# Sliding-window attention with ALiBi, then an ELU feed-forward: the order of the first steps, the layout of q and k, and the store of the last 128 rows

## Chip, core and metric

One NeuronCore of a Trainium2 chip runs the whole program. The metric is the device time of one execution in microseconds (us); lower is better. TensorE (PE) does the matmuls, VectorE (DVE), ScalarE (ACT) and GpSimd (POOL) the elementwise work, and SyncE (SP) issues some of the DMAs.

## The reference, cut to what matters

```python
# q, k, v: [8 batches, 8 heads, 576 positions, 64], f32; w_in [512, 2048]; w_out [2048, 512]
scores = (q @ k.T) / 8
rel  = pos[:, None] - pos[None, :]
bias = slopes[head] * -abs(rel)               # slopes = 2 ** -(head + 1) for 8 heads
mask = (rel >= 0) & (rel < 128)               # each query sees itself and the 127 keys before it
attn = softmax(where(mask, scores + bias, -1e9))
x = (attn @ v), heads side by side            # [4608 tokens, 512]
h = x @ w_in                                  # [4608, 2048]
g = where(h > 0, h, exp(min(h, 0)) - 1)       # ELU
out = g @ w_out                               # [4608, 512], f32
```

## The kernel before

**Tiling.** A batch has 576 positions: four blocks of 128 and a tail of 64. Because of the window a block of queries needs only its own block of keys and the one before it. Positions inside the first 512 are permuted by the load, so that long runs of memory land on each partition. All inputs come in on POOL's DMA queue and are cast to f16 on the way. Scores are computed with keys on the partitions and queries on the free axis, so their exponentials can serve directly as the stationary operand of the matmul with v; v carries a column of ones (`VW = D + 2`), which gives the softmax denominators.

**Layout.** `QK[i]` (two buffers, by the batch's parity) holds q and k with the head dimension on partitions 0 to 63: `[128, 2, 5, H, 128]`, that is q or k, then block, then head, then position. Partitions 64 to 127 hold extra rows of terms, the same for all batches, whose products add the ALiBi bias and large negative numbers outside the window. They are made once in `QK[1]` (`terms` L235 to L245 and `group_rows` L249 to L254 make `TQ` and `TK`; `fill_q` L257 on ACT, `fill_k` L261 on POOL and `k_term` L266 on DVE spread them over the heads) and are copied to `QK[0]` by one DMA (`fill_other` L270). Batch 0 does not wait for them: its scores use 64 rows only and add the bias by a second matmul of `cI` with `DM` (L372).

**Attention in banks.** A batch is 16 steps. `scores(b, s)` fills one PSUM bank (L352), and ACT takes its exponential (L376); for batches from 1 on DVE then clips outside the window (`cut`, L384); `values(b, s)` multiplies with v one step later (L398); `normalize` divides (L418, L419); `turn` brings the result into `xT`, with tokens on the free axis (L432 and L434 for batches 0 and 1, a transposing DMA after that).

**How q and k get into QK.** Batch 0 is loaded in two halves of 256 positions (`load_half`, L90), and each half is transposed on PE for four heads at a time (`transposes_half`, L291): `transposes_half(a, hq)` is half `a`, heads `4 hq` to `4 hq + 3`, 16 transposes, 8 of k and 8 of q. Batch 1 is loaded whole (`load_qk`, L83) and transposed for two heads at a time (`transposes`, L310, four calls at steps 13, 14, 15, 15). `put` (L300) copies each of these PSUM tiles into QK in two copies, both by one engine: DVE, or ACT where the last argument is true. Later batches go through DVE's 32x32 transpose (`squares`, L321) and gathering DMAs of SP (`collect`, L327). The 64 tail positions of each batch come by `load_tail` (L104, one DMA for k and one for q) and go through `transposes_tail` (L335, copies L340); for batch 0 that is in step 12, for batch 1 in step 25.

**Feed-forward.** It runs behind the attention in the same loop over steps. `hidden` computes 512 columns of `x @ w_in` (L455), ACT takes exp (L459), POOL limits it to at most 1 (L460); `elu` combines both on DVE one step later (L467); `output` accumulates `g @ w_out` (L496), ACT copies the bank (L500), SP stores it (L502). Each bank of hidden values is used by every second step, so `hidden` of step s + 2 waits for `elu` of step s. The first `hidden` is in step 4, the first `output` in step 13.

**Order.** It is written out by hand (`tc.manual_schedule()`): `at(s, f, ...)` appends `f` to step s, and the loop at the end emits, for each step, `hidden`, `elu` of the bank before, the tasks in the order in which they were appended, and `output`. Every engine runs its own instructions in that order. `warm(n)` (L509) issues n matmuls on the identity that nobody reads. Before step 0 stand `warm(34)`, the transposes of batch 0's first half for all heads, `warm(12)`, and `place_v4(0, 0)` (L119, DVE copies of v); each of steps 1 to 4 begins with `warm(8)`. `place_by_pool` (L124) does the rest of v's placing on POOL.

**POOL's DMA order.** Ahead of the loop: k, q (half 0), v (half 0), w_in 0 and 1, k, q (half 1), v (half 1), w_in 2 and 3, w_out 0 and 1. In the loop: k of batch 1 (step 4), q of batch 1 (step 5), w_out 2 and 3 (steps 6 and 7), tail of k and tail of q of batch 0 (steps 8 and 9), tail of v of batch 0 (step 10), v of batch 1 (step 11), and so on.

**The end.** The last four groups of 128 rows (`output` with t = 8) run on PE alone once the hidden values are done. The last group's 128 rows lie in three pieces of the output (`rows_of`: 32, 32 and 64 rows), so SP issues three stores after ACT's last copy.

Of the kernel before, what the change touches and what calls it, by code (L numbers as in the profile page):

```python
# [19 lines left out]
def kernel(  # L20
# [48 lines left out]
    QK = [one([128, 2, 5, H, 128], F16, f"QK{i}") for i in range(2)]  # L69
# [69 lines left out]
    with tc.manual_schedule():  # L139
# [68 lines left out]
        def zeros():  # L208
            for i in range(2):
                V.memset(QK[i][0:64 + 64 * i, 1, 4, :, 64:128], 0.0)  # L210
                V.memset(VP[i][64:128, 4, :, 0:D], 0.0)
            for e in EX:
                V.memset(e[:, 512:576], 0.0)
# [19 lines left out]
        def terms():  # L233

            V.tensor_scalar(out=is96, in0=rowf, scalar1=96.0, scalar2=None, op0=ALU.is_equal)  # L235
            V.tensor_scalar(out=is97, in0=rowf, scalar1=97.0, scalar2=None, op0=ALU.is_equal)
            V.tensor_scalar(out=isx, in0=is97, scalar1=-1.0, scalar2=None, op0=ALU.mult)
            V.tensor_scalar(out=pm[r_, :], in0=posi[r_, :], scalar1=float(-MID), scalar2=None,
                            op0=ALU.add)
            V.tensor_scalar(out=TQ[r_, 0:576], in0=pm[r_, :], scalar1=isx[r_, :], scalar2=is96[r_, :],  # L240
                            op0=ALU.mult, op1=ALU.add)
            V.tensor_scalar(out=TK[r_, 0:576], in0=pm[r_, :], scalar1=is96[r_, :],
                            scalar2=is97[r_, :], op0=ALU.mult, op1=ALU.add)
            for t in (TQ, TK):
                V.memset(t[64:128, 576:640], 0.0)  # L245
# [10 lines left out]
        def fill_q(n):  # L256
            nc.scalar.copy(QK[1][64:128, 0, n, :, :],  # L257
                           TQ[64:128, 128 * n:128 * n + 128].unsqueeze(1).broadcast_to([64, H, 128]))

        def fill_k(n):  # L260
            nc.gpsimd.tensor_scalar(  # L261
                out=QK[1][g_, 1, n, :, :], in0=TK[g_, 128 * n:128 * n + 128].unsqueeze(1)
                .broadcast_to([32, H, 128]), scalar1=1.0, scalar2=0.0, op0=ALU.mult, op1=ALU.add)

        def k_term(h):
            V.tensor_scalar(out=QK[1][r_, 1, :, h, :], in0=TK[r_, :].rearrange("p (n c) -> p n c", c=128),  # L266
                            scalar1=8.0 * 2.0 ** (-8.0 * (h + 1) / H), scalar2=None, op0=ALU.mult)
# [13 lines left out]
        def transposes_half(a, hq):  # L281

            if a:
                t = ps_o.tile([128, 2, 2, 4, 2, 32], F16, name="tph", tag="op")
            else:
                t = ps_s.tile([128, 2, 2, 4, 2, 32], F16, name="tp", tag="sps")
            p = slice(64 * a, 64 * a + 64)
            for w in (1, 0):
                for g in range(4):
                    for j in range(2):  # L290
                        nc.tensor.transpose(  # L291
                            t[:, w, :, g, j, :],
                            stq[0][p, w, 4 * hq + g, 2 * j:2 * j + 2, :].rearrange("p a d -> p (a d)"),
                            ident[p, p])
            put(t, QK[0][0:64, :, 2 * a:2 * a + 2, 4 * hq:4 * hq + 4, :], hq and not a)

        def put(t, o, by_act):

            for odd in range(2):
                (nc.scalar.copy if by_act else V.tensor_copy)(  # L300
                    o.rearrange("p w n h (a o i) -> p w n h a o i", o=2, i=32)[:, :, :, :, :, odd, :]
                    .rearrange("p w n h a i -> p w n (h a) i"),
                    t[64 * odd:64 * odd + 64].rearrange("p w n h a i -> p w n (h a) i"))

        def transposes(b, hp):
            t = ps_s.tile([128, 2, 4, 2, 2, 32], F16, name="tp", tag="sps")
            for g in range(2):
                for w in (1, 0):
                    for j in range(2):
                        nc.tensor.transpose(  # L310
                            t[:, w, :, g, j, :],
                            stq[b][:, w, 2 * hp + g, 2 * j:2 * j + 2, :].rearrange("p a d -> p (a d)"),
                            ident)
            put(t, QK[b % 2][0:64, :, 0:4, 2 * hp:2 * hp + 2, :], hp % 2)

        def squares(b, n):
# [4 lines left out]
            V.transpose(out=tt[b][:, w, dh, hs, :, :].rearrange("p h j i -> p (h j) i"),  # L321
                        in_=stq[b][:, w, hs, :, 32 * dh:32 * dh + 32].rearrange("p h j d -> p (h j) d"))

        def collect(b, n):

            dh, i = divmod(n, 4)
            nc.sync.dma_start(  # L327
                QK[b % 2][32 * dh:32 * dh + 32, :, i, :, :].rearrange("p w h c -> p w (h c)"),
                tt[b][32 * i:32 * i + 32, :, dh, :, :, :].rearrange("p w h j i -> p w (h j i)"))

        def transposes_tail(b):
# [7 lines left out]
            for g in range(2):  # L339
                V.tensor_copy(  # L340
                    QK[b % 2][0:64, :, 4, :, 0:64].rearrange("p w (n g) c -> p w n g c", g=2)[:, :, :, g, :],
                    t[64 * g:64 * g + 64, :, :, :])

        def scores(b, s):
# [6 lines left out]
            def mm(o, h, kc, qc, n):  # L351
                nc.tensor.matmul(t[:, o:o + n], qk[0:r, 1, kc, h, :], qk[0:r, 0, qc, h, 0:n],  # L352
# [133 lines left out]
        def output(t, j):  # L486

            ts, f0 = j // 4, 4 * (j % 4)
            last = t == NTB - 1
            if f0 == 0:  # L490
# [7 lines left out]
            if f0 == 12:  # L498
                ob = work.tile([128, DO], F32, name="ob", tag="ob")
                nc.scalar.copy(ob, ops[t])  # L500
                for p0, rows in rows_of(512 * t + 128 * ts):
                    nc.sync.dma_start(rows, ob[p0:p0 + rows.shape[0], :])  # L502

# [20 lines left out]
        transposes_half(0, 1)  # L524
        warm(12)
        for i in range(1, 5):
            at(i, warm, 8)
        place_v4(0, 0)

        for b in range(B):  # L530
            s0 = 16 * b
            for s in range(16):
                i, p = BANKS[s]
                half = p if i in (0, 4) else p // 2
                at(s0 + s, scores, b, s)
# [33 lines left out]
        at(5, terms)  # L569
# [69 lines left out]
```

## Time and profile before

| | |
|---|---|
| median of 5 runs | 358.35 us (358.11 to 359.75) |
| the profiled execution, time / span | 358.35 us / 356.6 us |
| PE busy | 332.3 us (93% of the span) |
| DVE / POOL / ACT busy | 250.1 / 215.2 / 187.6 us |
| POOL's DMA queue / SP's | 18.35 MB / 20.59 MB |
| matmuls of `warm` | 78, 9.1 us |

The span is what the profiler sees from the first to the last instruction; 1.75 us of the execution lie around it. PE is the busiest engine, but its share is not even: over most of the second half it is at 100%, in the first 80 us it is at 85% (67.9 us busy). The page cuts the span in 40 slices of 8.9 us. In its groups, `out<-in` are the tiles that an instruction writes and reads, and "idle before, releaser" says what ended the engine's idle time. The chain of waits follows the work that ended last back to its causes; the timeline lists the instructions in order of time; the table of windows gives each engine's busy time in chosen stretches, with the clock that TensorE was granted (1.00 is full) and what the DMA engines moved.

### The profile page before, as it was taken

How to read it: one execution, taken by the hardware profiler on the slowest of the kernel's cores; microseconds unless marked ns; L12 is line 12 of the kernel's file. 1: busy time of each engine (PE TensorE's matmuls, PEld its weight loads, DVE VectorE, ACT ScalarE, POOL GpSimd, SP SyncE). 2: the span in 40 equal slices, each digit the busy share in tenths (PEclk: the TensorE clock that was granted, in tenths of full speed). 3: DMA queues.
4: the chain of work that ended last, by engine and by line, in shares of the span. 5: the costliest groups of instructions: out<-in, count | busy, mean ns of one | idle time of the engine just before them, and what ended most of it. 6: DMA issues, size and time to landing. Idle time of an engine off the chain costs nothing.

```text
span 356.6 us, 9267 instructions
## 1 busy us (share of the span) xinstructions
PE 332.3 (93%) x3582; PEld 242.2 (68%) x3582; DVE 250.1 (70%) x565; ACT 187.6 (53%) x328; POOL 215.2 (60%) x332
## 2 busy tenths in 40 slices
PE   6988898889989989899999999999999999999994
PEld 6767676666666667667776777677777777666651
DVE  5559797498679688958895889588977667443330
ACT  3444767645455555555665565555555655444431
POOL 9265975988948955894688368936842322333320
PEclk9998999999999999999999999999999999999999
DMA  8999893658994597489749955993541222121122
GB/s 110 198 207 201 92 161 57 97 84 148 195 160 105 85 203 116 89 131 173 113 104 149 149 105 109 154 183 63 118 105 39 62 46 45 39 52 39 29 53 67
DMA packets 67435, 39.53 MB, mean 111 GB/s; under 512 B 30976, under 2 KB 59648, under 8 KB 67328
## 3 DMA queue, kind: packets, MB, share of 16 engines
q0 software_dynamic: 41904, 18.35, 45.2%
q1 hardware_dynamic: 25488, 20.59, 26.0%
q8 instruction: 28, 0.46, 0.6%
q14 instruction: 15, 0.12, 0.1%
HBM read 36.70 MB, written 9.44 MB: 129 GB/s over the span
## 4 chain that ended last, share of the span: by engine, by line
PE 60%; POOL 18%; DVE 9%; ACT 5%; issue 4%; DMA 2%; SPq 1%; ACTq 0%; POOLq 0%
PE hp L455 25%; PE op L496 22%; POOL VP L124 9%; POOL e L460 6%; PE sp L352 5%; PE av L398 4%; DVE g L467 3%; DVE tt L321 2%; DVE EX L384 2%; ACT e L459 1%; ACT EX L376 1%; DMA stq<-in_q_dram 1%; PE sp L372 1%; POOL stt L104 1%; DMA out_dram<-ob 1%
## 5 line engine op out<-in xcount | busy, mean ns | idle before, releaser
L460 POOL TENSOR_SCALAR e<-e 128x512 f32<-128x512 f32 x144 | 88.4, 614 | 116.9 <-ACT e L459 112.3
L455 PE MATMUL hp<-xT,wi 128*128 128x256 f16 (+3 forms) x1536 | 151.1, 247 | 7.4 <-DVE g L467 5.7
L455 PEld LDWEIGHTS <-wi 128*128 128x128 f16 x1536 | 122.3, 98 | 48.0 <-issue 8.0
L459 ACT ACTIVATE e<-hp 128x512 f32<-128x512 f32 x144 | 86.1, 598 | 126.9 <-PE hp L455 118.8
L496 PE MATMUL op<-wo,g 128*128 128x512 f16 x576 | 146.4, 379 | 0.4 <-ACT ob L500 0.4
L467 DVE SCALAR_TENSOR_TENSOR g<-e,hp 128x512 f16<-128x512 f32 x144 | 96.8, 673 | 42.0 <-POOL e L460 40.6
L376 ACT ACTIVATE EX<-sp 128x512 f16<-128x512 f32 x128 | 76.0, 593 | 18.8 <-PE sp L372 10.1
L124 POOL TENSOR_SCALAR VP<-vs 32x512 f16<-32x512 f16 x116 | 75.1, 647 | 7.8
L384 DVE TENSOR_TENSOR EX<-EX,band 128x512 f16<-128x512 f16 x112 | 55.0, 491 | 34.1 <-ACT EX L376 33.5
L496 PEld LDWEIGHTS <-g 128*128 128x128 f16 x576 | 51.2, 98 | 37.4 <-issue 0.5
L352 PE MATMUL sp<-QK 128*128 128x128 f16 (+3 forms) x576 | 50.5, 215 | 1.7 <-ACT QK L300 0.7
L398 PE MATMUL av<-VP,EX 128*128 128x65 f16 x576 | 39.1, 195 | 6.7 <-DVE EX L384 5.0
L398 PEld LDWEIGHTS <-EX 128*128 128x128 f16 x576 | 30.8, 98 | 13.7 <-DVE EX L384 9.2
L419 DVE TENSOR_TENSOR xn<-av,rden 128x256 f16<-128x256 f32 x80 | 34.0, 425 | 2.8
L352 PEld LDWEIGHTS <-QK 128*128 128x128 f16 (+1 forms) x576 | 31.8, 98 | 2.9 <-issue 0.9
L321 DVE STREAM_TRANSPOSE tt<-stq 128x512 f16<-128x512 f16 x48 | 33.1, 696 | 0.9 <-DMA QK<-tt 0.9
L500 ACT COPY ob<-op 128x512 f32<-128x512 f32 x36 | 21.1, 587 | 12.5 <-DMA out_dram<-ob 5.9
L418 DVE RECIPROCAL rden<-av 128x4 f32<-128x4 f32 x80 | 13.9, 174 | 7.9 <-PE av L398 7.2
L509 PE MATMUL spare<-ident 128*128 128x128 f16 x78 | 9.1, 303 | 1.6 <-DVE ident L165 1.6
L509 PEld LDWEIGHTS <-ident 128*128 128x128 f16 x78 | 8.0, 143 | 1.8 <-DVE ident L165 1.6
L300 ACT COPY QK<-tp 64x1024 f16<-64x1024 f16 x6 | 6.0, 1006 | 5.9 <-PE tp L291 5.2
L372 PE MATMUL sp<-DM,cI 128*128 128x256 f16 (+1 forms) x40 | 7.0, 282 | 0.0
(70 smaller groups left out, 125.2 us busy)
## 6 DMA issues: line engine op xcount, KB each, us to landing
out_dram<-ob SPq DMA_DIRECT2D x128, 64.0 KB, 1.8
QK<-tt SPq DMA_DIRECT2D x48, 128.0 KB, 2.5
stq<-in_k_dram POOLq DMA_DIRECT2D x7, 512.0 KB, 7.4
stq<-in_q_dram POOLq DMA_DIRECT2D x7, 512.0 KB, 8.7
vs<-in_v_dram POOLq DMA_DIRECT2D x7, 512.0 KB, 9.6
wi<-in_moe_w_in_dram POOLq DMA_DIRECT2D x4, 512.0 KB, 12.3
wo<-in_moe_w_out_dram POOLq DMA_DIRECT2D x4, 512.0 KB, 14.0
QK<-QK SPq DMA_DIRECT2D x1, 1280.0 KB, 8.8
```

What stands on the lines that cost most here:

```text
L124: nc.gpsimd.tensor_scalar(out=VP[b % 2][32 * j:32 * j + 32, n, :, 0:D], in0=vs[b][32 * n:32 * n + 32, :, j, :], scalar1=1.0, scalar2=0.0, ...
L321: V.transpose(out=tt[b][:, w, dh, hs, :, :].rearrange("p h j i -> p (h j) i"), in_=stq[b][:, w, hs, :, 32 * dh:32 * dh + 32].rearrange("p ...
L352: nc.tensor.matmul(t[:, o:o + n], qk[0:r, 1, kc, h, :], qk[0:r, 0, qc, h, 0:n], start=b > 0 or o == 0, stop=b > 0)
L376: nc.scalar.activation(e[:, 0:512], t, AF.Exp, scale=0.125)
L384: V.tensor_tensor(out=e, in0=e, in1=band[:, c:c + n].unsqueeze(1).broadcast_to([128, 512 // n, n]), op=ALU.min)
L398: nc.tensor.matmul(a[:, l, :], e[:, c:c + 128], vp[:, n, h, 0:D + 1], start=st, stop=sp)
L419: V.tensor_tensor(out=xnt[b, i][:, 4 * half:4 * half + 4, :], in0=a[:, :, 0:D], in1=r.unsqueeze(2).broadcast_to([128, 4, D]), op=ALU.mult)
L455: nc.tensor.matmul(p[:, l * w + u0:l * w + u1], w_in_sb[:, c, fc * 128:(fc + 1) * 128], xT[:, c, x0:x0 + u1 - u0], start=(c == 0), stop=(c ...
L459: nc.scalar.activation(e, p, AF.Exp)
L460: nc.gpsimd.tensor_scalar(out=e, in0=e, scalar1=1.0, scalar2=0.0, op0=ALU.min, op1=ALU.max)
L467: V.scalar_tensor_tensor(out=gs[t][:, f0:f0 + nf, c0:c0 + w], in0=sh(es.pop((t, j))), scalar=1.0, in1=sh(hps.pop((t, j))), op0=ALU.subtrac ...
L496: nc.tensor.matmul(ops[t], gs[t][:, fc, ts * 128:(ts + 1) * 128], w_out_sb[:, fc, :], start=(fc == 0), stop=(fc == NFC - 1))
```

## The change

The change has four parts.

1. **The start.** `QK` becomes `[128, 5, 2, H, 128]`: block, then q or k. `put` now gives every PSUM tile's even 32-column groups to DVE and the odd ones to ACT, and `transposes_half` calls it once for each of its two blocks, with copies of 64x512. Ahead of step 0 only the first four heads of the first half are transposed, and then `warm(8)` follows. The first scores, the other four heads' transposes, `warm(12)` and `place_v4(0, 0)` move into step 0; the second scores stand at the head of step 1, with `warm(12)` behind them. `warm` issues 90 matmuls in all.
2. **Layout.** All users of `QK` follow the new index order; `transposes`' PSUM tile and `squares`' tile `tt` are reordered too, and `collect` writes one run of 4 KB per partition where it wrote two of 2 KB.
3. **ALiBi terms.** The eight instructions of `terms` go from DVE to POOL, and from step 5 to the end of step 0.
4. **The last 128 rows** are computed by `output_end` in two halves of 256 columns, each with 16 matmuls of 256 columns. The first half is copied by ACT, the second half by DVE and ACT with 128 columns each. The three stores of each half are shared between SP's and ACT's DMA queues.

```diff
-    QK = [one([128, 2, 5, H, 128], F16, f"QK{i}") for i in range(2)]
+    QK = [one([128, 5, 2, H, 128], F16, f"QK{i}") for i in range(2)]
...
         def terms():
-            V.tensor_scalar(out=is96, in0=rowf, scalar1=96.0, scalar2=None, op0=ALU.is_equal)
+            nc.gpsimd.tensor_scalar(out=is96, in0=rowf, scalar1=96.0, scalar2=None, op0=ALU.is_equal)
...
             for t in (TQ, TK):
-                V.memset(t[64:128, 576:640], 0.0)
+                nc.gpsimd.memset(t[64:128, 576:640], 0.0)
...
-            put(t, QK[0][0:64, :, 2 * a:2 * a + 2, 4 * hq:4 * hq + 4, :], hq and not a)
-
-        def put(t, o, by_act):
-
-            for odd in range(2):
-                (nc.scalar.copy if by_act else V.tensor_copy)(
-                    o.rearrange("p w n h (a o i) -> p w n h a o i", o=2, i=32)[:, :, :, :, :, odd, :]
-                    .rearrange("p w n h a i -> p w n (h a) i"),
-                    t[64 * odd:64 * odd + 64].rearrange("p w n h a i -> p w n (h a) i"))
+            for n in range(2):
+                put(t[:, :, n], QK[0][0:64, 2 * a + n, :, 4 * hq:4 * hq + 4, :])
+
+        def put(t, o):
+
+            s = "n w h" if len(o.shape) == 5 else "w h"
+            f = s.replace("w h", "w (h a)")
+            for odd, copy in enumerate((V.tensor_copy, nc.scalar.copy)):
+                r = o.rearrange(f"p {s} (a o i) -> p {s} a o i", o=2, i=32)
+                r = r[:, :, :, :, :, odd, :] if len(o.shape) == 5 else r[:, :, :, :, odd, :]
+                copy(r.rearrange(f"p {s} a i -> p {f} i"),
+                     t[64 * odd:64 * odd + 64].rearrange(f"p {s} a i -> p {f} i"))
...
-            put(t, QK[b % 2][0:64, :, 0:4, 2 * hp:2 * hp + 2, :], hp % 2)
+            put(t, QK[b % 2][0:64, 0:4, :, 2 * hp:2 * hp + 2, :])
...
-                QK[b % 2][32 * dh:32 * dh + 32, :, i, :, :].rearrange("p w h c -> p w (h c)"),
-                tt[b][32 * i:32 * i + 32, :, dh, :, :, :].rearrange("p w h j i -> p w (h j i)"))
+                QK[b % 2][32 * dh:32 * dh + 32, i, :, :, :].rearrange("p w h c -> p (w h c)"),
+                tt[b][32 * i:32 * i + 32, dh, :, :, :, :].rearrange("p w h j i -> p (w h j i)"))
...
             last = t == NTB - 1
+            if last and ts == 3:
+                return output_end(j % 4)
...
+        def output_end(k):
+
+            half, f0 = k // 2, 8 * (k % 2)
+            c = slice(256 * half, 256 * half + 256)
+            if f0 == 0:
+                ops[half] = (ps_s if half else ps_o).tile([128, DO], F32, name=f"end{half}",
+                                                         tag="sps" if half else "op")
+            for fc in range(f0, f0 + 8):
+                nc.tensor.matmul(ops[half][:, 0:256], gs[NTB - 1][:, fc, 384:512], w_out_sb[:, fc, c],
+                                 start=(fc == 0), stop=(fc == NFC - 1))
+            if f0:
+                ob = work.tile([128, 256], F32, name=f"obe{half}", tag="ob")
+                if half:
+                    V.tensor_copy(ob[:, 0:128], ops[half][:, 0:128])
+                nc.scalar.copy(ob[:, 128 * half:256], ops[half][:, 128 * half:256])
+                for n, (p0, rows) in enumerate(rows_of(NTOK - 128)):
+                    (nc.scalar if n == 1 or n + half == 2 else nc.sync).dma_start(
+                        rows[:, c], ob[p0:p0 + rows.shape[0], :])
...
         warm(34)
         transposes_half(0, 0)
-        transposes_half(0, 1)
-        warm(12)
-        for i in range(1, 5):
+        warm(8)
+        at(0, scores, 0, 0)
+        at(0, transposes_half, 0, 1)
+        at(0, warm, 12)
+        at(0, place_v4, 0, 0)
+        at(1, scores, 0, 1)
+        at(1, warm, 12)
+        for i in (2, 3, 4):
             at(i, warm, 8)
-        place_v4(0, 0)
...
-                at(s0 + s, scores, b, s)
+                if b or s > 1:
+                    at(s0 + s, scores, b, s)
...
-        at(5, terms)
+        at(0, terms)
```

## The prediction

> **What bounds the kernel now.** I read the page first, then the chain of waits, the table of windows, the DMA view, and the timeline around the steps that the change touches.
>
> ```profile
> PE 332.3 (93%) x3582; PEld 242.2 (68%) x3582; DVE 250.1 (70%) x565; ACT 187.6 (53%) x328; POOL 215.2 (60%) x332
> ```
>
> PE bounds the second half (20.00 of every 20 us from 240 on), so what is won earlier survives only if it is still there when PE becomes the bound. The chain of waits shows what sets the pace at the start:
>
> ```profile
> 9.91 1.02 ACT QK L300
> ...
> 10.97 0.58 PE sp L352 x4
> ...
> 16.43 0.85 PE spare L509 x8
> ...
> 19.18 0.45 PE spare L509 x8
> ...
> 24.42 0.77 DVE pm L238
> ...
> 26.86 0.70 DVE g L467
> 27.57 0.04 issue
> 27.61 1.87 PE hp L455 x16
> ```
>
> The first scores wait for ACT's slow copies (1.0 us each). The same eight warming matmuls take 0.85 us at 16.43 and 0.45 at 19.18: PE runs at half clock until about 17.5. From 24.09 `terms` occupies DVE ahead of `elu`, and PE stands until 27.61. The windows show what that standing costs, and what DMA does meanwhile (columns: PE, PEld, DVE, ACT, POOL busy, clock, DMA share, GB/s):
>
> ```profile
> 24.30:27.70 3.40, 1.23 (x24) 0.89 (x23) 3.24 (x9) 0.60 (x2) 3.18 (x5) 0.96 1.26 205
> 27.70:31.10 3.40, 3.40 (x34) 3.04 (x34) 3.32 (x8) 0.60 (x1) 0.94 (x3) 0.54 1.43 198
> 31.10:34.50 3.40, 3.12 (x50) 2.50 (x47) 3.27 (x11) 2.13 (x4) 2.25 (x4) 1.00 1.36 203
> 34.50:38.00 3.50, 3.01 (x47) 2.62 (x46) 3.18 (x10) 2.74 (x5) 3.22 (x6) 1.00 1.32 202
> 38.00:41.40 3.40, 2.58 (x41) 2.10 (x38) 1.90 (x4) 1.79 (x4) 3.11 (x5) 1.00 0.56 46
> ```
>
> After a stretch with PE busy 1.23 of 3.40 us the clock falls to half for one stretch of 3.4 us. And the DMA engines move some 200 GB/s without a gap until 38 us: POOL's queue never runs empty, whatever the other engines do. The last thing in that backlog which PE needs is the tail of q for batch 0:
>
> ```profile
> 36.18 0.73 POOL L104 DMA_DIRECT2D stt<-in_q_dram  x1
> ...
> 41.83 0.40 PE L335 MATMUL tpt<-ident,stt 64*128 64x64 f16 x8
> ```
>
> ```profile
> stt<-in_q_dram POOLq DMA_DIRECT2D x1, 64.0 KB, 4.4
> ```
>
> It is issued at 36.18 and lands 4.4 us later, at 40.6; `transposes_tail(0)` uses it at 41.83, only 1.2 us after. Issuing it earlier brings it no nearer: ahead of it stand 6 loads of 256 KB, 8 of weights and 2 of 512 KB, 6.8 MB, which at 200 GB/s from 4 us last until 38, and then two tails in small packets. So the start can bring PE at most 1.2 us.
>
> **The change part by part.**
>
> *The first scores.* Eight transposes of q end at 7.9. A copy of 64x512 costs about 0.42 us on DVE (xT<-xps, 512 columns) and 0.59 on ACT (the exponential of 512), against 0.69 and 1.01 of a 64x1024 one, so block 0 is in place at 8.6, and behind `warm(8)` the scores start near 8.8, not 10.97. Moved along are the 16 other transposes (1.0 us at half clock) and DVE's `place_v4`, which ends near 13.1 and which nobody needs before. But `warm` grows by 12 matmuls, 12 x 0.107 = 1.3 us: summing PE's work from 7.40 at half clock, the third scores come at 15.8, where they now come at 15.35. A gain needs the clock to open earlier. PE has no hole left from 7.40 on (it stood 0.7 us before 10.97), so I expect that one stretch of 3.4 us earlier; then the first `hidden` starts near 17.2, not 18.29; without it near 18.8.
>
> *Terms.* On DVE 2.8 us disappear ahead of `elu` at 24.09. On POOL nothing shows these forms: between the nearest rows, 0.61 us (v's placing, 32x512) and DVE's own 0.75, three large ones cost about 2.1 us, five small ones at 0.1 to 0.25 another 0.8, 2.9 in all, 2.5 to 4.5 with gaps. They stand behind POOL's second w_out issue, which ends at 13.48, and ahead of L460, which starts at 19.91 after 6.4 us of idle: free. If that cover were gone, the load of k and the first L460 would be late by as much.
>
> *Transposes of batch 0's second half* (steps 5 and 6): DVE loses 2 x 0.69 and gets 2 x 0.42, ACT gets 2 x 0.59, in a stretch where ACT is busy 0.60 of 3.40. Together with `terms` PE's stop before 27.61 (2.17 us) and the half clock behind it (1.7 us) go. What is late next is `hidden` 7's w_in, landing 15.5 us after 8.6, at 24.1, and then POOL: from 19.91 to its L460 of step 10, ending 38.96, it idles 0.63 + 2.46 + 1.08 us, leaving 14.9 of work. Begun at 18.8 (17.2 + matmuls 0.9 + ACT 0.6) it ends at 33.7; with `elu`, `hidden` 12 and the scores (0.7 + 0.9 + 0.8) PE reaches the tail's transposes near 36.5, up to 38.5 if the clock opens late.
>
> *There it waits until 40.65, the wall from here on.* **The start's 5 us shrink to 41.83 - 40.65 = 1.2.** Behind PE's waiting transposes stand DVE's tail copies L340, then `hidden` 13 and all of step 13; POOL runs on to step 12's work and stops.
>
> *Its price.* PE idles 2.2 to 4.1 us. The trace's case: 2.17 us idle, one stretch at half clock. Half clock after 40.65 counts in full, for PE is the bound there (4.00 of 4.00 us busy at 44 to 48). Depending on where the stretches lie, between 0.7 and 1.7 us are lost; I take 1.4. [...] The row decides: a stretch 36% busy was enough.
>
> *Batch 1's transposes.* ACT's work by call is now 0, 2.0, 0, 2.0 us and will be 1.0 each. At step 15 it matters:
>
> ```profile
> 51.85 2.03 ACT L300 COPY QK<-tp 64x1024 f16<-64x1024 f16 x2 [0.69 <-PE tp L310]
> 53.89 1.04 ACT L257 COPY QK<-TQ 64x1024 f16<-64x1024 f16 x1
> 54.95 0.60 ACT L459 ACTIVATE e<-hp 128x512 f32<-128x512 f32 x1
> ...
> 56.65 0.30 PE L398 MATMUL av<-VP,EX 128*128 128x65 f16 x4 [0.64 <-DVE EX L384]
> ```
>
> The two calls' copies can start at 51.17, right after the exponential, and end at 53.2, not 53.88; L257, L459 and the exponential follow 0.7 us earlier, and PE's wait of 0.64 goes. I take 0.6 (0 if DVE's `cut` is late instead). POOL's chain, which sets the pace from 59.72, starts from there.
>
> *Layout.* `fill_q`, `fill_k`, `k_term` and the matmul operands keep their sizes: nothing. `collect` writes the same 128 KB in half as many runs; PE and DVE wait for it 1.3 + 0.9 us in all (QK<-tt), so -0.3 to +0.3, taken as 0. SP idles around it.
>
> *The end.* PE's time stays: 32 matmuls of 256 columns at 0.109 us (L455's pitch) for 16 at 0.216, weight loads of 0.098 beside them. Today:
>
> ```profile
> 351.92 0.59 ACT L500 COPY ob<-op 128x512 f32<-128x512 f32 x1 [2.87 <-DMA out_dram<-ob]
> 352.53 1.30 SPq L502 DMA_DIRECT2D out_dram<-ob  x3
> ```
>
> A copy of 128 columns is about 0.30 us on either engine (ACT's cI rows, 128 columns: 0.295), so 0.29 less. SP then issues two stores, not three: 0.42 + 0.04 less. ACT's issue is nowhere in the trace: at least SP's 0.32, at most POOL's 0.93; I take SP's 0.4, the same kind of plain store. The first half's two ACT issues end by 351.5, ahead of ACT's last copy; at 0.93 they would make it late by 0.6. A first use of SP's queue (56.54) landed in 1.7 us, so I add nothing for ACT's first. Sum -0.75, between -1.0 and 0; I take -0.8.
>
> **Sum.** -1.2 (start, up to the wall) + 1.4 (clock) - 0.6 - 0.8 = -1.2 us. The profiled execution took 358.35, span 356.6 and 1.75 around it, which is also the median: 357.1.
>
> **The rivals.**
>
> [...]
>
> *The wall does not hold*: the tail lands with its issue, and the start's gain of some 5 us comes through: -4.8 - 1.4 = 352.1. Against it: 200 GB/s without a gap.
>
> *Slower: the clock stays low.* The place is step 12 to 15, where scores, transposes of batch 1 and `output` alternate with waits for ACT; were these stretches not dense enough, each further one at half clock costs 1.7 us. One more gives 358.8; from the second on the kernel is slower: 360.5. Against it: behind the fall at 27.70 the next stretch was granted in full.
>
> *It doesn't do what it says*: the scores could still wait for ACT's second block, 9.2 rather than 8.6. The wall swallows that too.
>
> **How the numbers follow.** Wall and clock together 0.62 at 357.1 (own range 356.0 to 358.8: the clock's 0.7 to 1.7 or one more stretch, ACT's 0 to 0.7, the end's 0 to 1.0); no fall 0.19; no wall 0.07; clock stays low 0.12. This kernel's measurement tells 0.3%, 1.07 us, from no change: faster is below 357.28. Of the first case a little over half lies below it: 0.35 + 0.19 + 0.07 = 0.61 faster, 0.26 the same, 0.13 slower. From 355.2 to 359.2 no more than the last two cases are left out.
>
> **What would show it.** The first scores near 8.8; full pitch of matmuls by 14 to 15; no stop before `hidden` 7 beyond its weights; L335 at 40.6 to 41 after an idle PE released by DMA stt; a half-clock stretch between 39 and 46; L459 of step 16 earlier against step 15 by 0.7; a last copy of 0.3 us and two SP stores behind it. If L335 comes before 40, the wall was wrong; if the clock stays full, the second case holds.

## The result, and the profile after

| | before | changed |
|---|---|---|
| median | 358.14 us (80 runs) | 357.14 us (43 runs) |
| ratio, 95% interval | | 0.9975 (0.9966 to 0.9984) |
| profiled execution, time / span | 358.35 / 356.6 us | 356.81 / 355.0 us |
| tail's transposes of batch 0 start | 41.83 us (L335) | 41.22 us (L338) |
| from there to the end of the span | 314.7 us | 313.8 us |

The changed kernel is faster by 0.25%, some 0.9 us. The two profiled executions differ by 1.54 us, which is the difference of two single runs; the steps below are read from them, the size of the gain from the ratio. The prediction said 357.1 us. The number is right; of the terms behind it the two largest are not, and the end's is half its size.

The chain of waits of the changed kernel, up to the place where the prediction put the wall:

```profile
8.09 0.59 ACT QK L305
8.72 0.61 PE sp L355 x4
...
16.26 0.75 DVE VP L119
...
18.04 0.28 PE xps L435 x2
...
19.10 0.89 PE hp L458 x16
...
28.52 0.62 POOL VP L124
29.18 0.28 PE av L401 x4
...
35.26 5.91 DMA stt<-in_q_dram
41.22 0.40 PE tpt L338 x8
```

The first scores start at 8.72, as forecast (8.8). What they win is gone by the first `hidden` (19.10 in this view, 18.29 before): the chain runs through DVE's copies of v at 16.26. From 35.26 it is one piece, the load of the tail of q, issued at 35.26 and landing 5.91 us later. So the wall is there, and the chain passes through it. But PE came to it late, as its own timeline shows:

```profile
39.13 1.05 PE L458 MATMUL hp<-xT,wi 128*128 128x128 f16 x16 [0.82 <-DVE xT L437]
...
41.22 0.40 PE L338 MATMUL tpt<-ident,stt 64*128 64x64 f16 x8 [0.26 <-DMA stt<-in_q_dram]
```

So PE arrived at 40.96 and waited for the DMA 0.26 us, where 2.2 to 4.1 had been forecast. The windows (same columns as before) show no half clock behind it:

```profile
36.00:40.00 4.00, 3.02 (x46) 2.61 (x46) 2.69 (x8) 2.15 (x3) 3.60 (x6) 1.00 1.16 141
40.00:44.00 4.00, 3.74 (x58) 2.95 (x56) 3.26 (x8) 3.34 (x5) 3.82 (x5) 1.00 0.75 67
44.00:48.00 4.00, 4.00 (x57) 3.08 (x55) 3.87 (x9) 2.62 (x5) 3.56 (x6) 1.00 1.27 146
```

Where PE lost its lead is in ACT's and POOL's timelines. ACT at the copies of batch 0's second half:

```profile
23.97 0.58 ACT L305 COPY QK<-tph 64x512 f16<-64x512 f16 x1 [0.36 <-DVE QK L305]
25.04 0.58 ACT L305 COPY QK<-tph 64x512 f16<-64x512 f16 x1 [0.48 <-DVE QK L305]
25.65 0.60 ACT L462 ACTIVATE e<-hp 128x512 f32<-128x512 f32 x1
```

POOL at `terms` and at L463 of steps 4, 5, 6, 8 and 10:

```profile
13.31 0.41 POOL L235 TENSOR_SCALAR is<-rowf 128x1 f32<-128x1 f32 x1
...
14.13 1.67 POOL L238 TENSOR_SCALAR pm<-posi 32x576 f32<-32x576 int32 x1
...
20.80 0.61 POOL L463 TENSOR_SCALAR e<-e 128x512 f32<-128x512 f32 x1 [2.66 <-ACT e L462]
...
22.84 0.60 POOL L463 TENSOR_SCALAR e<-e 128x512 f32<-128x512 f32 x1 [0.51 <-ACT e L462]
...
26.40 0.61 POOL L463 TENSOR_SCALAR e<-e 128x512 f32<-128x512 f32 x1 [0.73 <-ACT e L462]
...
31.80 0.60 POOL L463 TENSOR_SCALAR e<-e 128x512 f32<-128x512 f32 x1 [1.16 <-ACT e L462]
...
37.41 0.61 POOL L463 TENSOR_SCALAR e<-e 128x512 f32<-128x512 f32 x1
```

ACT's copies wait for DVE's copies of the same PSUM bank, and DVE's for ACT's: the two take turns. The four copies take from 23.52 to 25.62, 2.1 us, where DVE alone took 1.38, and ACT's exponential of `hidden` 6 stands behind them. Side by side, ACT's two copies of 0.58 us, begun at 23.52, would have ended near 24.7. The traces put the turns with the PSUM bank that both read and not with `QK`, which both write: where the two engines copy different PSUM tiles into the same `QK`, as here for batch 1, their copies overlap (DVE's from 51.11 to 51.79 beside ACT's from 50.92 to 52.84).

```profile
50.92 1.92 ACT L305 COPY QK<-tp 64x1024 f16<-64x1024 f16 x2 [0.51 <-DVE QK L305]
51.11 0.68 DVE L305 COPY QK<-tp 64x1024 f16<-64x1024 f16 x1 [0.22 <-PE tp L313]
```

`terms` runs on POOL from 13.31 to 18.15, 4.8 us, ahead of a stop that lasts until 20.80. That is longer than forecast, and it makes none of POOL's own work late; but it is not free, as the experiment that undoes it shows.

The end, in the timeline of the changed kernel:

```profile
349.70 2.54 SPq L525 DMA_DIRECT2D out_dram<-obe  x3
350.78 0.29 DVE L522 COPY obe<-end 128x128 f32<-128x128 f32 x1 [6.72 <-DMA out_dram<-ob]
351.10 0.27 ACT L523 COPY obe<-end 128x128 f32<-128x128 f32 x1 [1.71 <-DVE obe L522]
351.40 0.37 ACTq L525 DMA_DIRECT2D out_dram<-obe  x1
```

Here too ACT waits for DVE. The last issue ends at 352.24, 1.55 us behind PE's last matmul (350.69), where before it was 353.83 against 351.84, 2.0.

### The profile page after: what moved, and what is told of

It is laid out like the page before. It is cut to its first block, busy times and chain, and to the rows that moved or that the text cites. A ratio compares the mean times of both kernels' runs of the same rounds, so it can differ in the third digit from the quotient of the medians.

```text
span 355.0 us, 9347 instructions
## 1 busy us (share of the span) xinstructions
PE 330.4 (93%) x3610; PEld 241.8 (68%) x3610; DVE 247.9 (70%) x560; ACT 190.1 (54%) x335; POOL 219.4 (62%) x340
## 4 chain that ended last, share of the span: by engine, by line
PE 60%; POOL 16%; DVE 10%; ACT 4%; issue 4%; DMA 4%; SPq 1%; ACTq 0%; POOLq 0%
PE hp L458 25%; PE op L501 23%; POOL VP L124 8%; PE sp L355 5%; POOL e L463 5%; PE av L401 4%; DVE g L470 2%; DVE tt L324 2%; DMA out_dram<-ob 2%; DMA stt<-in_q_dram 2%; DVE EX L387 2%; ACT e L462 2%; ACT EX L379 1%; POOL stt L104 1%; PE sp L375 1%
## 5 line engine op out<-in xcount | busy, mean ns | idle before, releaser
L463 POOL TENSOR_SCALAR e<-e 128x512 f32<-128x512 f32 x144 | 88.4, 614 | 111.3 <-ACT e L462 103.2
L501 PE MATMUL op<-wo,g 128*128 128x512 f16 x560 | 142.9, 379 | 0.4 <-ACT ob L505 0.4
L470 DVE SCALAR_TENSOR_TENSOR g<-e,hp 128x512 f16<-128x512 f32 x144 | 96.8, 672 | 42.2 <-POOL e L463 41.9
L501 PEld LDWEIGHTS <-g 128*128 128x128 f16 x560 | 49.7, 98 | 35.5 <-issue 0.5
L401 PEld LDWEIGHTS <-EX 128*128 128x128 f16 x576 | 30.8, 98 | 15.1 <-DVE EX L387 8.9
L305 ACT COPY QK<-tp 64x512 f16<-64x512 f16 (+1 forms) x8 | 6.3, 796 | 8.0 <-DVE QK L305 8.0
L305 DVE COPY QK<-tp 64x512 f16<-64x512 f16 (+1 forms) x8 | 4.4, 547 | 3.4 <-PE tp L291 1.8
```

The costliest lines, as they stand in the source:

```text
L401: nc.tensor.matmul(a[:, l, :], e[:, c:c + 128], vp[:, n, h, 0:D + 1], start=st, stop=sp)
L463: nc.gpsimd.tensor_scalar(out=e, in0=e, scalar1=1.0, scalar2=0.0, op0=ALU.min, op1=ALU.max)
L470: V.scalar_tensor_tensor(out=gs[t][:, f0:f0 + nf, c0:c0 + w], in0=sh(es.pop((t, j))), scalar=1.0, in1=sh(hps.pop((t, j))), op0=ALU.subtrac ...
L501: nc.tensor.matmul(ops[t], gs[t][:, fc, ts * 128:(ts + 1) * 128], w_out_sb[:, fc, :], start=(fc == 0), stop=(fc == NFC - 1))
```

## The experiments

Theories. *Wall*: PE can't pass the tail's transposes before the tail of q has landed; what the start wins ahead of it is lost in the wait. *Rival*: there is no wall that matters, each repaired step shows in the time. Beside these stand the prices of the single parts.

### The end alone

```diff
 # before, with the changed kernel's output_end
+            if last and ts == 3:
+                return output_end(j % 4)
```

> The kernel before with part 4 alone: the last 128 rows in two column halves. The prediction's sum says 0.8 us less than before (ratio 0.9978). Rival, read from the two traces: DVE's and ACT's copies of the second half come one after the other, not side by side, so the last store is issued 1.5 us behind PE's last matmul instead of 2.0 and the gain is 0.4 to 0.5 us (0.9987). Nothing ahead of 343 us differs from before.

Measured: 0.9995 (0.9979 to 1.0010). The interval takes in both theories, so the time does not decide. From the start of the tail's transposes (42.07) to the end of the span it takes 314.5 us, 0.3 less than before; the copies' turns are those of the fence above (0.29, then 0.27). The last issue ends 1.5 us behind PE. The timeline speaks for the rival, 0.4 to 0.5 us.

### DVE's copies of v a step earlier

```diff
+        at(0, place_v4, 0, 1)
...
-        at(1, place_v4, 0, 1)
```

> The changed kernel with DVE's second four copies of v (place_v4(0, 1)) in step 0 instead of step 1, so that they no longer stand ahead of the second normalize. The first hidden matmuls should start near 17.6 to 18.1 us instead of 18.94. Theory (the tail of q is a wall): the tail's transposes L338 still start at about 41.2, PE waits longer for them, and the time is that of the changed kernel, 0.9975 of before, or up to 1.7 us more if PE's wait grows enough for the clock to fall. Rival (the order of the steps decides, no wall): everything behind comes about 1.2 us earlier, ratio 0.994.

Measured: 0.9965 (0.9956 to 0.9975). PE's timeline:

```profile
17.93 1.06 PE L458 MATMUL hp<-xT,wi 128*128 128x128 f16 x16
...
40.51 0.40 PE L338 MATMUL tpt<-ident,stt 64*128 64x64 f16 x8 [0.55 <-DMA stt<-in_q_dram]
```

The first `hidden` comes 1.0 us earlier, but only half of that is the copies' doing. From the third scores to the first `hidden` it takes 3.00 us (14.93 to 17.93), in the changed kernel 3.51 (15.43 to 18.94). The third scores themselves come 0.50 us earlier because in this execution PE is at full pitch sooner: four matmuls of `values` at 14.13 take 0.29 us here, and 0.43 at 14.38 in the changed kernel. At the tail PE waits longer than in the changed kernel and gets 0.7 us, all that this execution's earlier landing (40.5, not 41.2) allowed.

### The same, with the tails ahead of the last w_out

```diff
-        at(6, load_wo, 2, 1)
-        at(7, load_wo, 3, 1)
+        at(8, load_wo, 2, 1)
+        at(9, load_wo, 3, 1)
...
-            at(8 + i, load_tail, 0, w)
+            at(6 + i, load_tail, 0, w)
```

> As e2_early_place, and in POOL's order the two tails of batch 0 change places with the last two loads of w_out (steps 6 and 7 against 8 and 9): POOL issues as much in each step, but 1 MB less stands ahead of the tails, some 5 us. Theory (wall): the tails land near 36, L338 starts with the steps ahead of it, at 39.7 to 40.3, and the time falls 0.9 to 1.5 us below e2_early_place, ratio 0.9935 to 0.995. Rival (no wall): the same as e2_early_place, whatever that is.

Measured: 0.9966 (0.9954 to 0.9978), the same as without the swap: the theory's number is missed. The profile says why this run can't decide. The wait for DMA is gone from L338, but PE arrives only at 40.55, because the clock fell earlier. Its timeline, and its windows:

```profile
28.04 0.28 PE L401 MATMUL av<-VP,EX 128*128 128x65 f16 x4 [1.60 <-POOL VP L124]
...
28.81 1.64 PE L458 MATMUL hp<-xT,wi 128*128 128x128 f16 x16
```

```profile
24.00:28.00 4.00, 2.10 (x38) 1.77 (x37) 3.13 (x8) 3.40 (x6) 3.13 (x5) 1.00 1.28 205
28.00:32.00 4.00, 3.96 (x41) 3.37 (x41) 2.96 (x11) 1.35 (x3) 2.06 (x4) 0.64 1.45 198
```

PE's stop of 1.60 us for POOL's copies of v was followed by a stretch at half clock (0.64 on average over 28 to 32).

### The swap alone

The second half of the diff above, on the changed kernel.

> The changed kernel with the swap of the tails and the last two loads of w_out alone. Theory: the changed kernel's PE waits for the tail of q by 0.3 to 0.5 us only, so L338 starts at 40.8 instead of 41.22 and the time falls by 0.3 to 0.5 us, ratio near 0.9963. Rival (the order of the steps decides, no wall): no change, 0.9975.

Measured: 0.9986 (0.9973 to 1.0000); no gain, so the theory's 0.9963 falls. L338 starts at 41.26 without any wait for DMA: in this execution the first `hidden` came at 19.16, and PE's own pace brought it there no sooner. In the changed kernel the wall and PE's pace lie together within half a microsecond; taking away the wall alone shows nothing.

### Terms alone, and terms undone

```diff
 # before, with the changed kernel's terms
-        at(5, terms)
+        at(0, terms)
```

> The kernel before with part 3 alone: terms on POOL in step 0. Theory A (the terms are the part of the start that pays): PE's stop before hidden 7 (2.2 us at 27.61) goes, hidden 7 starts with its weights near 24.5, no half-clock stretch follows, and PE comes to the tail's transposes L335 no later than the tail of q lands, 40.5 to 41.2 instead of 41.83: 0.6 to 1.3 us less than before, ratio 0.9965 to 0.998. Theory B (DVE's copies and the scores matter, the terms only fill DVE while it would wait anyway): ratio above 0.999.

Measured: 1.0000 (0.9980 to 1.0019), which is theory B's number; of theory A only the upper edge is left. But PE's timeline in the profiled execution (357.11 us) follows theory A:

```profile
25.36 1.07 PE L455 MATMUL hp<-xT,wi 128*128 128x128 f16 x16
...
40.55 0.40 PE L335 MATMUL tpt<-ident,stt 64*128 64x64 f16 x8 [1.09 <-DMA stt<-in_q_dram]
```

`hidden` 7 starts at 25.36, not 27.61, PE meets the wall and waits there for 1.09 us. The 14 runs spread from 356.2 to 360.2 us: the profile is one of the fast ones. Six of the seven slowest have a mean granted clock of 0.981 to 0.985, the profiled one has 1.00, so a fall of the clock in a part of them would fit; where it fell these runs don't show.

The other way round, the changed kernel with its terms on DVE in step 5:

> The changed kernel with part 3 undone: terms on DVE in step 5. Theory A: PE stops again before hidden 7, for 2 to 3 us, often with a half-clock stretch behind it, and L338 comes 1 to 2.5 us later than in the changed kernel; time 0.8 to 2 us above it, ratio 1.000 to 1.003. Theory B: within 0.3 us of the changed kernel, 0.9975.

Measured: 0.9999 (0.9987 to 1.0011), the number of theory A's lower end: without part 3 nothing of the gain is left. PE's timeline shows the old stop, and a `hidden` 7 at half clock behind it:

```profile
27.63 1.60 PE L458 MATMUL hp<-xT,wi 128*128 128x128 f16 x16 [2.05 <-DVE g L470]
```

L338 starts at 42.13, 0.9 us later than in the changed kernel.

The run shows a cost of the terms, too. DVE's second four copies of v, in the changed kernel and then here:

```profile
15.52 1.80 DVE L119 COPY VP<-vs 32x512 f16<-32x512 f16 x4
```

```profile
15.43 1.18 DVE L119 COPY VP<-vs 32x512 f16<-32x512 f16 x4
```

With POOL idle beside them the same copies take 0.62 us less, and from the third scores to the first `hidden` it takes 3.01 us (15.22 to 18.23) in place of 3.51.

### DVE alone for the second half of batch 0

```diff
+            if a:
+                o = QK[0][0:64, 2:4, :, 4 * hq:4 * hq + 4, :]
+                for odd in range(2):
+                    V.tensor_copy(
+                        o.rearrange("p n w h (a o i) -> p w n h a o i", o=2, i=32)[:, :, :, :, :, odd, :]
+                        .rearrange("p w n h a i -> p w n (h a) i"),
+                        t[64 * odd:64 * odd + 64].rearrange("p w n h a i -> p w n (h a) i"))
+                return
             for n in range(2):
                 put(t[:, :, n], QK[0][0:64, 2 * a + n, :, 4 * hq:4 * hq + 4, :])
```

> The changed kernel with the copies of batch 0's second half (steps 5 and 6) by DVE alone, two of 64x1024 as before. In the changed kernel DVE and ACT take turns on a PSUM bank (0.42 + 0.59 + 0.42 + 0.59 us), which holds up ACT's exponential of hidden 6, POOL's instructions behind it and its copies of v, for which PE stands 1.66 us before 29.18. Theory C (taking turns is the cause of that stop): hidden 8 starts about 1 us earlier, at 28.6 to 29.0 instead of 29.95, PE reaches the tail's transposes earlier and waits there for the tail of q, so the time falls by 0.3 to 0.7 us only, ratio 0.9955 to 0.9967. Rival (POOL alone sets that stop): hidden 8 within 0.3 us of 29.95, ratio 0.9975.

Measured: 0.9947 (0.9930 to 0.9964), better than the changed kernel. PE's stop for POOL's copies of v is shorter, 1.07 us in place of 1.66; in PE's timeline `hidden` 8 starts 0.8 us earlier, though this execution's first `hidden` (18.76) was only 0.2 earlier, and PE meets the wall:

```profile
28.37 0.28 PE L409 MATMUL av<-VP,EX 128*128 128x65 f16 x4 [1.07 <-POOL VP L124]
...
29.14 1.06 PE L466 MATMUL hp<-xT,wi 128*128 128x128 f16 x16
...
40.58 0.40 PE L346 MATMUL tpt<-ident,stt 64*128 64x64 f16 x8 [0.47 <-DMA stt<-in_q_dram]
```

Theory C holds for 0.6 us of that stop: sharing a bank between two engines made this copy slower, and the delay went on through ACT's exponential and POOL to PE. The other 1.07 us stay with DVE alone, and the kernel before with part 3 alone has the same stop (1.07 us before 27.73): that much is POOL's chain itself. The run takes ACT's share of the copies away together with the turns; that the turns are the larger part of it rests on the sum above (25.62 in place of 24.7).

### Batch 1's copies by one engine each

```diff
-            put(t, QK[b % 2][0:64, 0:4, :, 2 * hp:2 * hp + 2, :])
+            o = QK[b % 2][0:64, 0:4, :, 2 * hp:2 * hp + 2, :]
+            for odd in range(2):
+                (nc.scalar.copy if hp % 2 else V.tensor_copy)(
+                    o.rearrange("p n w h (a o i) -> p w n h a o i", o=2, i=32)[:, :, :, :, :, odd, :]
+                    .rearrange("p w n h a i -> p w n (h a) i"),
+                    t[64 * odd:64 * odd + 64].rearrange("p w n h a i -> p w n (h a) i"))
```

> The changed kernel with batch 1's four transposes copied by one engine each (DVE, ACT, DVE, ACT), as before. Theory: ACT's exponential L462 of step 16 comes 0.4 to 0.6 us later, counted from the tail's transposes L338 (12.7 us behind them in the changed kernel, 13.1 before), and PE's wait for the clipping ahead of values(1, 0) grows from 0.33 to 0.65 us: 0.4 us more, ratio 0.9985. Rival (what is won there is lost again in POOL's chain): 0.9975.

Measured: 0.9968 (0.9957 to 0.9980), not to be told from the changed kernel's 0.9975: 0.4 us is at the edge of what the time can tell. ACT's timeline has the step itself:

```profile
51.69 2.03 ACT L319 COPY QK<-tp 64x1024 f16<-64x1024 f16 x2 [0.69 <-PE tp L313]
53.73 1.04 ACT L257 COPY QK<-TQ 64x1024 f16<-64x1024 f16 x1
54.79 0.60 ACT L467 ACTIVATE e<-hp 128x512 f32<-128x512 f32 x1
```

The tail's transposes start at 41.67 here, so step 16's exponential stands 13.12 us behind them, as before (54.95 - 41.83), against 12.70 in the changed kernel (53.92 - 41.22): part 1 is worth 0.42 us at this place.

### Both repairs, without and with the swap

The two diffs of DVE's copies together, on the changed kernel:

> The changed kernel with both repairs: DVE's second four copies of v in step 0, and the copies of batch 0's second half by DVE alone. Each alone brought PE to the wait for the tail of q at 40.5 (waits 0.55 and 0.47 us). Theory (wall): hidden 12 starts near 37.3, PE waits 1.2 to 1.6 us, L338's place stays 40.5, the time is no lower than with either repair alone, 0.9947 to 0.9965 of before, and above that if the clock falls during the wait. Rival (no wall): 1 us below e7_half1_dve, 0.992 to 0.993.

Measured: 0.9953 (0.9934 to 0.9972), no better than the second repair alone: the wall's number, not the rival's. PE's timeline and the windows of the profiled execution (359.03 us, the slowest of 22; the fastest took 355.45):

```profile
37.54 1.05 PE L466 MATMUL hp<-xT,wi 128*128 128x128 f16 x16 [0.82 <-DVE xT L445]
...
41.91 0.40 PE L346 MATMUL tpt<-ident,stt 64*128 64x64 f16 x8 [2.55 <-DMA stt<-in_q_dram]
42.25 1.47 PE L466 MATMUL hp<-xT,wi 128*128 128x128 f16 x16
```

```profile
40.00:44.00 4.00, 2.09 (x30) 1.95 (x31) 1.87 (x5) 1.35 (x3) 2.27 (x3) 0.84 1.16 133
44.00:48.00 4.00, 4.00 (x42) 3.00 (x41) 2.84 (x6) 2.02 (x4) 2.16 (x3) 0.73 0.59 52
```

This is the prediction's chain of events, in a kernel that does reach the wall early: 2.55 us of waiting, then a stretch at half clock (0.84 and 0.73 on average). From L346 to the `hidden` of step 16 (54.01) it takes 12.1 us, against 10.55 in the changed kernel (41.22 to 51.77): the fall costs 1.55 us.

The fall comes only in some executions. The 22 runs lie in two groups: 14 from 355.45 to 356.56 us, all with a mean granted clock of 0.989 or more, and 8 from 357.26 to 359.03, six of them with 0.985 or 0.986. The profiled one is of the second group.

With the swap:

> As e9_place_and_half1, with the tails of q and k issued ahead of the last two loads of w_out. Theory (wall): the tails land near 36, L338 starts at 39.0 to 39.5 without a wait for DMA, 1.2 us earlier than without the swap, and the time falls by as much, ratio 0.991 to 0.9935. Rival: POOL's chain from 57 on takes it back, and the ratio is that of e9_place_and_half1.

Measured: 0.9896 (0.9862 to 0.9930), median 355.10 us, the fastest of all kernels run here. PE's timeline:

```profile
39.09 0.40 PE L346 MATMUL tpt<-ident,stt 64*128 64x64 f16 x8
```

No wait for DMA, and 2.1 us earlier than in the changed kernel. Between this kernel and the one above only the order of four loads on POOL's queue differs. That shows the wall: once PE comes early, it is the tail's place in the queue that decides. Of the 1.27 us between the two medians some 0.8 is the wait (against the faster group above, whose median is 355.89), the rest the fall: an estimate from these times.

### A tail that comes late

```diff
-            at(8 + i, load_tail, 0, w)
+            if w:
+                at(8, load_tail, 0, w)
...
         at(11, load_v4, 1)
+        at(11, load_tail, 0, 0)
```

> The changed kernel with the tail of q for batch 0 issued three steps later, behind v of batch 1 (512 KB): PE must wait at L338 for 3 to 4 us, as the prediction had it. It tests the price that the prediction put on such a wait. Theory (the trace's row of before, 2.17 us were enough): the granted clock falls to half for at least one stretch of 3.4 us within 40 to 50, on top of the wait itself (3.4 us): 4.2 to 5.3 us more than the changed kernel, ratio 1.009 to 1.013. [...]

Measured: 1.0169 (1.0117 to 1.0221), more than the theory's 1.009 to 1.013, because the tail landed later than I had reckoned:

```profile
47.21 0.60 PE L338 MATMUL tpt<-ident,stt 64*128 64x64 f16 x8 [6.03 <-DMA stt<-in_q_dram]
```

```profile
39.71:43.12 3.41, 1.47 (x23) 1.03 (x20) 1.71 (x5) 2.29 (x4) 3.25 (x6) 1.00 0.47 32
43.12:46.54 3.42, 0.00 (x0) 0.00 (x0) 0.00 (x0) 0.00 (x0) 1.76 (x2) 0.50 1.45 165
46.54:49.95 3.41, 2.74 (x30) 2.56 (x31) 2.02 (x5) 0.28 (x1) 0.00 (x0) 0.50 0.28 21
49.95:53.36 3.41, 3.41 (x19) 1.99 (x18) 1.89 (x4) 1.73 (x3) 2.15 (x3) 0.50 0.14 12
```

L338 is 6.0 us later than in the changed kernel, and PE runs at half clock (0.50) from there until about 53.4, which costs another 3.1 us, half of that time, as an estimate; the profiled executions differ by 8.8. The price of the wait was so, in this run, the wait itself and about half of the half-clock time behind it. PE's last matmul before the wait ended at 41.18, and the clock fell at 43.12, behind 1.9 us of idle time, at the end of a stretch in which PE had been busy for 1.47 of 3.41 us.

### The last half by DVE alone

```diff
-                if half:
-                    V.tensor_copy(ob[:, 0:128], ops[half][:, 0:128])
-                nc.scalar.copy(ob[:, 128 * half:256], ops[half][:, 128 * half:256])
+                (V.tensor_copy if half else nc.scalar.copy)(ob, ops[half][:, 0:256])
```

> As e9_with_swap, and the second half of the last rows is copied by DVE alone, 256 columns, instead of 128 by DVE and then 128 by ACT. Theory (DVE and ACT take turns on the bank, 0.29 + 0.03 + 0.27 us): one copy of about 0.42 us, so the last issue ends 0.15 to 0.2 us earlier behind PE's last matmul. Rival: no difference there. Both are below what the time can tell; the timeline decides. The time is that of e9_with_swap.

Measured: 0.9902 (0.9869 to 0.9936), the same as with the swap. The timeline decides: DVE's one copy starts at 349.35 and takes 0.42 us, the last issue ends at 350.64, 1.38 us behind PE's last matmul (349.26); with two engines it was 1.55 (350.31 against 348.76). One engine is 0.17 us quicker here than two that take turns.

## Why the prediction was right, and where it was not

**The sum.** -1.2 (start) + 1.4 (clock) - 0.6 (batch 1's copies) - 0.8 (end) had been forecast. Between the profiled executions it was -0.6, 0, -0.42 and -0.44, together -1.5. That the number came out is luck in part: start and clock together were forecast as +0.2 and were -0.6, the other two as -1.4 and were -0.86, and the two errors, of opposite sign, took each other back. By the prediction's own sign, a clock that stays full, its second case should have held, without the 1.4 us of the clock (357.1 - 1.4 = 355.7 us); the profiled execution shows no fall at the wall (1.00 from 36 to 48) and took 356.81.

**The first scores: right in time.** 8.72 us, and full pitch of the matmuls from about 15.1, a tenth behind the forecast 14 to 15. The way there was another: in this execution the eight warming matmuls at 7.44 already ran at full pitch (0.62 us), and the granted clock then fell to half from 8.1 to 14.9. The forecast's reason, that the clock opens one stretch earlier because PE has no hole, does not describe this execution.

**The first hidden at 17.2: wrong.** The prediction looked at the four copies of `place_v4` that move to step 0, which indeed nobody needs before they end, and put the second four, left in step 1, at nothing. They now stand behind a normalize that comes later, and ahead of the next one, for which PE waited 1.34 us. Moving them shortens the way from the third scores to the first `hidden` by 0.5 us (3.51 to 3.00).

**Terms: two costs put too low.** 4.8 us on POOL, above the forecast's upper bound of 4.5, but still covered for POOL itself. What was put at nothing is DVE: its four copies of v beside them take 1.80 us in place of 1.18, and 0.5 us of this reaches the first `hidden`. The gain needs the other parts: undoing the terms takes the whole gain away (0.9999), and the terms alone bring none (1.0000).

**Batch 0's second half: wrong.** The prediction gave DVE two copies and ACT two and let them run side by side. They take turns, 2.1 us for 1.38. The stop before `hidden` 7 did go, but a new one of 1.66 us stands before `hidden` 8, behind POOL; 0.6 us of it comes from the turns. Giving the copies back to DVE was worth 0.9 us by the medians (357.14 to 356.26, on different chips), 0.28% by the ratios.

**The wall: right in kind, nearly idle in the changed kernel.** The forecast was an arrival at 36.5 to 38.5 and a landing at 40.65. PE arrived at 40.96 and the tail landed at 41.17. The step that failed is POOL's way to L463 of step 10: it was to begin at 18.8 and to work 14.9 us without a stop, until 33.7. Its work was 14.8 us, but it began at 20.80, behind the late first `hidden`, and stood 0.51, 0.73 and 1.16 us for ACT's exponentials, until 38.02. These 4.3 us are nearly the whole delay of PE. So the start's term is half its size, and the wait too short for the next term. That the wall is there was shown only with both repairs, where the swap of four loads brought the ratio from 0.9953 to 0.9896.

**The fall of the clock: right in kind, place wrong.** It did not happen behind 0.26 us. It did behind 2.55 us, for 1.55 us, inside the forecast 0.7 to 1.7. The prediction took it from one row of the kernel before, 2.17 us of waiting. The waits of 2.17 us, of 2.55 and, with the swap and the early copies, of 1.60 were each followed by a half-clock stretch (0.50 from 27.41 to 30.83; 0.73 on average over 44 to 48; 0.64 over 28 to 32). In these executions a stretch that was about half idle, or more, was enough.

How busy PE was ahead of a fall can be read from the windows and from PE's timeline. Behind a fall half clock lasted 3.41 us in the kernel before (27.41 to 30.83), twice that in the changed kernel (8.10 to 14.92) and three times that with the late tail (43.12 to 53.36). In the 3.41 us ahead of the fall PE had been busy for 1.29 us in the kernel before (24.00 to 27.41), for 1.80 in the changed kernel (4.69 to 8.10), for 1.47 with the late tail (39.71 to 43.12) and for 1.81 with the early copies and the swap. The clock stayed at 1.00 behind 1.81 us with the swap alone, and in the changed kernel behind 1.77 (59.29 to 62.71) and 2.02 (25.16 to 28.58). About half idle was so followed by half clock in some of these stretches and not in others; what decides between them is not shown.

The zero in the sum above holds for the profiled execution only. Of the 43 others the six with a mean granted clock of 1.00 took 356.4 to 357.4 us, and the 13 slowest, from 357.79 up, had 0.981 to 0.993: in some the clock fell once more. One such place is known. In two of the experiments (batch 1's copies by one engine each, and the late tail), which run the same instructions up to there, the clock fell at 29.4 and 29.5, behind the same stop of 1.66 us.

**Batch 1's copies: right**, 0.42 for 0.6. PE's wait for the clipping, 0.64 us, did not go but fell to 0.33. **The end: right in kind, half as much**, mostly because its two copies take turns too (0.59 us together, not 0.30). ACT's own issues, the unknown of that step, took 0.37 to 0.49 us, close to the 0.4 chosen.

**Layout: not tested alone.** PE's and DVE's waits for a gathering DMA (0.6 and 0.9 us before) are no longer in the profile; what that is worth in time is not shown.

## What to carry to other kernels

Ask of an early gain what arrives next by a clock of its own: here a load at the end of a queue, with the DMA engines moving some 200 GB/s without a gap (197 to 207 from 17.2 to 37.6 us in the kernel before), landed only behind that stretch, at 40.6, and what took PE's wait away was its place in the queue (2.55 us of waiting in one order, none in the other). Two engines that read one PSUM bank were not two engines here (2.1 us in turns, 1.38 by DVE alone): check in the timeline whether each copy's releaser is the other's copy, and count the latency of what stands behind them on both queues. Work moved to an idle engine can slow the engine beside it (DVE's copies of v 1.80 us in place of 1.18): look at what runs at that time. And where two limits lie together, one repair alone shows nothing or a little; it took three together here, 0.9896 against the changed kernel's 0.9975.

## What the runs showed of the hardware that was not expected

- DVE and ACT copying different partitions or columns of one PSUM bank wait for each other in this program: in the changed kernel ten of ACT's twelve copies waited for DVE's, 9.3 us in all, 4.4 of them ahead of the first copy. In these copies the halves lie on partitions 0 to 63 and 64 to 127, at the end on columns 0 to 127 and 128 to 255. Whether the chip would let the two read side by side is not shown.
- `terms` on POOL slows DVE's copies of v. The four copies of step 1 took 1.58 to 2.07 us in the six profiles in which `terms` ran on POOL beside them (the changed kernel, the swap alone, the terms alone, DVE alone for the second half, batch 1's copies, the late tail), and 1.18 in the three in which POOL was idle then (the kernel before, the end alone, the terms undone). Two of these pairs differ in nothing but the terms (1.80 and 1.18; 1.65 and 1.18). By what means POOL slows DVE is not shown.
- The tail of q landed between 40.5 us (the early copies) and 41.9 (both repairs) in executions whose queue was in the same order, so the wall itself moves by more than a microsecond.
- The same stop of PE can be followed by half clock or not. The 1.66 us before 29.18 in the changed kernel lie across the end of a stretch (PE busy for 2.02 of 3.42 us before it, for 2.81 of 3.41 behind it), and the clock stayed; in the two experiments with a fall at 29.4 and 29.5 they lie inside one (1.75 of 3.41 us busy). Inside a stretch it is still not certain: with 1.81 of 3.41 us the clock fell in the run with the early copies and the swap, and stayed in the run with the swap alone.
- The granted clock in the windows reads 1.00 ahead of a trace's first change of clock even where PE is slow: in the kernel before, eight warming matmuls at 14.05 take 1.06 us, and 0.61 at 19.02, and both read 1.00. At the start go by the pitch of the matmuls.
